# Softmax attention and linear attention on one core: another mark for the zero matmuls, the last normalisation ahead of the leftover steps, and VectorE's blocks at other places

## The chip, the core and the metric

One core of a Trainium2 chip runs the whole program: TensorE (PE in the profile) multiplies matrices, ScalarE (ACT) takes exponentials, VectorE (DVE) and GpSimd (POOL) do elementwise work, SyncE (SP) issues most of the transfers. The metric is the device time of one execution in microseconds (us). The kernel before takes 875.0 us, the median of 3 runs from 873.52 to 875.77.

## The reference

Two independent blocks with the same shapes, 2048 rows of 640 features, 32 heads of 20:

```python
qkv = (x @ wqkv)  ->  q, k, v per head
# A: softmax attention
p = softmax(q k^T * 20 ** -0.5);  o = p v;  a = o @ wo
# B: linear attention
phi(t) = where(t > 0, t + 1, exp(t)) + 1e-6
kv = phi(k)^T v;  z = sum(phi(k));  o = phi(q) kv / (phi(q) z + 1e-6);  b = o @ wo
out = concatenate([a, b], axis=-1)
```

All inputs and the output are bf16.

## The kernel before

**The units of A.** Block A is cut into 32 pieces n: 8 groups g of four heads, times 4 chunks of 512 queries (n = 4 g + chunk). Each n has 16 key tiles kt of 128 keys, and each tile four heads i, so that a unit (n, kt, i) is one score matmul (line 1193): 20 features by 128 keys by 512 queries, in one quarter of TensorE's rows, into one of the eight banks of TensorE's result memory (`ps`, 512 columns each). Its exponential is taken in one of two ways.

- On ScalarE: `emit_exp` (line 1250, the instruction is line 1259) takes three units at once from banks 0 to 2, then two from banks 3 and 4, in turn, and writes them to `f_PT`. There are 730 such groups; group j is the counter of the whole program.
- On VectorE: `ND[n]` says how many of the 16 key tiles of n go there, 56 in all. `d_score` (line 1281) evicts a score from bank 6 or 7 with a scale and an offset (line 1294); three polynomial passes over two units (lines 1305, 1309, 1313) give the exponential in `f_PD`. One key tile, a block, is four evictions and six passes.

**The output of A.** `pv_quad` (line 1344) multiplies the four exponentials of a key tile with `f_V` into bank 5 (`PVB`), four matmuls side by side, each in a quarter of the columns; 16 of them add up there for one n. A column of ones in `f_V` gives the sums. `norm` (line 1403) then transposes the bank on VectorE (line 1407), takes reciprocals (1414), multiplies on GpSimd (1417; for the last n on VectorE, 1420) and transposes back into `f_OTp` (1424); transfers (line 1436) lay it into `f_OTd`, from which `step_out` multiplies with `wo`. For the last n, `norm` keeps reciprocal, product and transposition in `self.norm_last`.

**The background.** Everything else is a list of steps: projections of A (`step_qk`, `step_v`), the whole of B (`b_steps`), and the output of A (`step_out`). A step takes bank 6 or 7, issues its matmuls piece by piece, and ends with an eviction. `bg` (line 985) issues pieces for as long as the planned end of TensorE's work lies ahead of `limit`, the planned end of the exponential of group j plus 0.12 us. Without credit it goes on only where `recent`, the planner's TensorE work in the last 3.41 us (a quarter of the array counts a quarter), is not above `FLOOR`.

**The planner.** All instructions are put in order while the program is built. `_Clock` (line 728) is a clock kept by hand with fixed costs; `run` (line 1832) goes through the 730 groups: scores of group j+1, a score for VectorE, exponential j, `emit_pv`, `bg`, `fill`, then whatever VectorE has left.

**The zero matmuls.** `zeros` (line 1197) puts a matmul with zero weights (`f_z`) beside the scores, in a quarter of the rows. `fill` (line 1216) puts sets of four, each in a quarter of the columns, up to 512 wide, into bank 5, where zeros add nothing. It stops when the room up to `limit` is used, or when `recent` is above `FLOOR`, and it does nothing where no product of the present n stands in bank 5 yet or where the bank isn't free. It runs for 2 < j < 725.

**The end.** `tail` (line 1942) issues the last products, then all steps that are left over; `finish_out` (line 1493) then issues products of `f_OTd` and `wo` (`part1`), calls `norm_last`, multiplies the last `f_OTp` with the last rows of `wo` (`part2`), adds on VectorE (line 1540) or copies on ScalarE (line 1536), and stores.

Of the kernel before, what the change touches and what calls it, by code (L numbers as in the profile page):

```python
# [5 lines left out]
F32 = mybir.dt.float32  # L6
# [793 lines left out]
class _Fast:  # L800
# [3 lines left out]
    AUX = (6, 7)  # L804
    NPT = 20
    NPD = 8
    FLOOR = 1.45
    GAP = 0.2
    BURST = True
    LEAD = 0.6  # L810
    LATE = ((3, 1), (3, 0), (2, 1))
    ND = (1, 2, 1, 1, 2, 2, 2, 2, 2, 2, 2, 2, 2, 2, 1, 2, 2, 2, 2, 2, 2, 1, 2, 1, 2, 2, 2, 2, 2, 1, 1, 2)
    OCT = 42
    EXP_A = -65536.0
    EXP_B = 3.8973859448844363 * 65536.0
# [4 lines left out]
    def __init__(self, nc, sch, es, ps, A_x, A_wqkv, A_wo, B_x, B_wqkv, B_wo, out):  # L820
        self.nc = nc
        self.sch = sch
        self.es = es
        self.ps = ps
        self.Ax, self.Aw, self.Awo = A_x, A_wqkv, A_wo
        self.Bx, self.Bw, self.Bwo = B_x, B_wqkv, B_wo
        self.out = out[0]
        self.S = A_x.shape[1]
        self.NQC = self.S // 512
        self.NT = self.S // 128  # L830
        self.prio = []
        self.qa = []
        self.qb = []
        self.qv = []
        self.done = {}
        self.cur = None
        self.open = set()
        self.ck = sch.clock = _Clock()
        self.acts = []
        self.dq = []  # L840
        self.last_chain, self.last_n = None, -1
        self.nq = []
        self.credit = 0
        self.j = -1
        self.brr = 0
        self.zj = {}
        self.aslot = self.bslot = 0
        self.hlo = []
        for c in range(N_DC):
            h0 = (128 * c) // D_HEAD  # L850
            h1 = min(N_HEADS - 1, (128 * c + 127) // D_HEAD)
            self.hlo.append((h0, h1 - h0 + 1))
# [4 lines left out]
    def alloc(self):  # L857
        S, NT = self.S, self.NT
        self.KT = self.sb("f_KT", [128, 2, S], BF16)
        self.Qr = self.sb("f_Qr", [128, 4, 512], BF16)  # L860
        self.V = self.sb("f_V", [128, NT, N_HEADS, 21], BF16)
        self.xT = self.sb("f_xT", [128, N_DC, S], BF16)
        self.wA = self.sb("f_wA", [128, N_DC, 3 * D_MODEL], BF16)
        self.wo = self.wA[:, :, 2 * D_MODEL:3 * D_MODEL]
        self.wo7 = self.sb("f_wo7", [128, D_MODEL], BF16)
        self.PT = self.sb("f_PT", [128, self.NPT, 512], BF16)
        self.PD = self.sb("f_PD", [128, self.NPD, 512], BF16)
        self.W = self.sb("f_W", [128, 2, 1024], F32)
        self.PL = self.sb("f_PL", [128, 2, 1024], F32)
        self.T1 = self.sb("f_T1", [128, 512], F32)  # L870
        self.Tn = self.sb("f_Tn", [128, 512], BF16)
        self.OTp = self.sb("f_OTp", [128, 512], BF16)
        self.R = self.sb("f_R", [128, 32], F32)
        self.OTd = self.sb("f_OTd", [128, N_DC, S], BF16)
        self.stage = self.sb("f_st", [128, 4, D_MODEL], BF16)
        self.wBq = self.sb("f_wBq", [128, N_DC, D_MODEL], BF16)
        self.wBkv = self.sb("f_wBkv", [128, N_DC, 2 * D_MODEL], BF16)
        self.woB = self.wBkv[:, :, 0:D_MODEL]
        self.pqT = self.wBkv[:, :, D_MODEL:D_MODEL + 512]
        self.xBt = self.sb("f_xB", [128, 2, N_DC, 512], BF16)  # L880
        self.xB = [self.xBt[:, k] for k in range(2)]
# [12 lines left out]
        self.Cs = self.sb("f_cs", [128, 2, 128], BF16)  # L894
        self.De = self.sb("f_de", [128, 16, 21], BF16)
        self.rd = self.sb("f_rd", [128, 2, 16], F32)
        self.Z = self.sb("f_z", [128, 128], BF16)
        self.G = self.sb("f_g", [128, 128], BF16)
        self.gmx = self.sb("f_gmx", [128, 8], F32)
        self.ident = self.sb("f_id", [128, 128], BF16)  # L900
        self.flag = self.sb("f_flag", [128, 1], I32)
        self.bmx = self.sb("f_bmx", [128, 1], F32)
        self.warm = self.sb("f_warm", [128, 1], F32)
        self.ones = self.sb("f_ones", [128, 1], F32)
# [309 lines left out]
                        self.G[32 * i:32 * (i + 1), :].unsqueeze(1).broadcast_to([32, 4, 128]), start=False, stop=False, reads=("Z", "G"), writes=(("ps", b),), tp=(32 * i, 0), inc=False, sgc=True)  # L1214

    def fill(self, limit):
        while self.pvcnt[min(self.pvn, self.NN - 1)] > 0:
            t = self.ck.pe_end()
            w = int(2400 * (limit - t - 0.1)) // 128 * 128
            if w <= 0 or self.ck.recent(limit) > self.FLOOR:  # L1220
                return
            if self.sch.when((), (("ps", self.PVB),), skip="pe") > t:
                return
            w = min(w, 512)
            for i in range(4):
                self.sch.mm(self.ps[32 * i:32 * (i + 1), self.PVB, 0:w], self.Z[:, 32 * i:32 * (i + 1)],
                            self.G[:].unsqueeze(1).broadcast_to([128, w // 128, 128]), start=False, stop=False, reads=("Z", "G"),
                            writes=(("ps", self.PVB),), tp=(0, 32 * i), inc=False, sgc=True)

    def force_qk(self, n, kt):  # L1230
        g, qc = divmod(n, self.NQC)
# [32 lines left out]
    def d_ready(self, slack):  # L1264
        k = self.dk
        if k >= len(self.dun):
            return None
        p = k // 2
        if p >= 2 and self.dC.get(p - 2) is None:
            return None  # L1270
        return self.bank(slack)

# [8 lines left out]
    def d_score(self, b):  # L1281
        sch, ps = self.sch, self.ps
        k = self.dk
        i = self.d_head()
        self.dk += 1
        n, kt, _ = self.dun[k]
        self.dhead.setdefault(k // 4, []).append(i)
        p, h = divmod(k, 2)
        x = p % 2
        self.score(b, n, kt, i, True)  # L1290
        cs = 128.0 / (LN2 * float(D_HEAD) ** 0.5)
        cb = 128.0 * (127 + self.OCT)
        dst = self.W[:, x, 512 * h:512 * (h + 1)]
        self.dve(0.69, lambda e: e.tensor_scalar(dst, ps[:, b, :], cs, cb, op0=ALU.mult, op1=ALU.add),  # L1294
                 reads=(("ps", b),), writes=(("W", x, h),))
        if h == 0:
            return
        w, pl = self.W[:, x, :], self.PL[:, x, :]
# [77 lines left out]
    def emit_pv(self, most, limit, last=False):  # L1376
        c = 0
        while c < most and self.pvn < self.NN:
# [8 lines left out]
            if left_d and self.pvcnt[n] > 0:  # L1387
                cj = self.dC.get(2 * self.pdnext + 1)
                if cj is not None and cj <= t:
                    self.pv_d()  # L1390
                    c += 1
                    continue
            if left_d and self.pvcnt[n] >= self.NT - 2 and (ok_a or not left_a):
                self.d_force(self.pdnext)
                self.pv_d()
                c += 1
                continue
# [5 lines left out]
    def norm(self, n):  # L1403
# [46 lines left out]
        if n == self.NN - 4:  # L1450
            for t in range(4 * (self.NQC - 1), 4 * self.NQC):
                for h in range(2):
                    if (t % 4, h) not in self.LATE:
                        self.prio.append(self.step_out(t, h, 1, (("OT", n), ("bkv", self.NQC - 1, 3))))

    def step_out(self, t, h, part, needs):
        sch, ps = self.sch, self.ps
        tl = t % 4
# [8 lines left out]
        def post(b):  # L1467
# [8 lines left out]
            if h == 0:  # L1476
                self.aslot ^= 1
            s = self.aslot
            dst = self.stage[:, s, cs]
            self.dve(0.49, lambda e: e.tensor_copy(dst, ps[:, b, 0:320]), reads=(("ps", b),),  # L1480
                     writes=(("stage", s, h),))
            if h == 1:
                sch.dma("sp", lambda e: e.dma_start(self.out[128 * t:128 * (t + 1), 0:D_MODEL],
                                                    self.stage[:, s, :]),
# [8 lines left out]
    def finish_out(self):  # L1493
# [15 lines left out]
                     self.wo7[:, 320 * h:320 * (h + 1)], x not in late, True, w7, banks[x], True)  # L1509
        for x in late[:2]:  # L1510
            part1(x)
        n = self.NN - 1
        self.norm_last(n)
        for x in tiles[:len(tiles) - len(late)]:
            part2(x)
        for x in late[:2]:
# [58 lines left out]
    def b_steps(self):  # L1575
# [162 lines left out]
        def ostep(t, h):  # L1738
# [8 lines left out]
            def post(b):  # L1747
                if h == 0:
                    self.bslot ^= 1
                s = 2 + self.bslot  # L1750
                dst = self.stage[:, s, 320 * h:320 * (h + 1)]
                self.dve(0.49, lambda e: e.tensor_copy(dst, ps[:, b, 0:320]), reads=(("ps", b),),  # L1752
                         writes=(("stage", s, h),))
                if h == 1:
                    sch.dma("sp", lambda e: e.dma_start(
                        self.out[128 * t:128 * (t + 1), D_MODEL:2 * D_MODEL], self.stage[:, s, :]),
                        reads=(("stage", s, 0), ("stage", s, 1)), writes=(("bout", t),))
# [184 lines left out]
    def tail(self, NG):  # L1942
        nq = len(self.quads)
        self.udone = 4 * nq
        while self.pvn < self.NN:
            self.j += 1
            self.run_acts(1e9)
            if self.pvn == self.NN - 1 and self.pvcnt[self.pvn] == self.NT - 1:
                while self.nq or self.dq:
                    if self.nq:  # L1950
                        self.nq.pop(0)[1]()
                    else:
                        self.d_pass()
            self.emit_pv(1, 1e9, True)
        while self.cur is not None or self.prio or self.qa or self.qv or self.qb or self.nq:
            self.j += 1
            self.run_acts(1e9)
# [91 lines left out]
```

## Time and profile before

| | |
|---|---|
| timed runs | 875.0 us (873.52 to 875.77) |
| the profiled execution | 870.45 us, its span 868.6 us |
| ScalarE busy | 850.2 us, 790 instructions |
| TensorE busy | 757.8 us, 11260 matmuls |
| VectorE busy | 751.2 us, 1036 instructions |
| mean granted TensorE clock | 0.996 |
| first exponential begins, last ends | 10.7 and 858.2 us |

The span runs from the first to the last instruction of one execution. A row of a group reads: line, engine, operation, written tile <- read tiles, shapes, count, then busy time in us and mean ns of one, then idle time of the engine just before these instructions and what ended it. A row of a stretch reads: from:to, its length, then the busy time of PE, PEld (weight load), DVE, ACT and POOL with counts, the granted clock, the share of the transfer engines and GB/s. A row of the chain reads start, length, engine, tile, line; one of the timeline start, length, engine, line, operation.

### The profile page before, as it was taken

How to read it: one execution, taken by the hardware profiler on the slowest of the kernel's cores; microseconds unless marked ns; L12 is line 12 of the kernel's file. 1: busy time of each engine (PE TensorE's matmuls, PEld its weight loads, DVE VectorE, ACT ScalarE, POOL GpSimd, SP SyncE). 2: the span in 40 equal slices, each digit the busy share in tenths (PEclk: the TensorE clock that was granted, in tenths of full speed). 3: DMA queues.
4: the chain of work that ended last, by engine and by line, in shares of the span. 5: the costliest groups of instructions: out<-in, count | busy, mean ns of one | idle time of the engine just before them, and what ended most of it. 6: DMA issues, size and time to landing. Idle time of an engine off the chain costs nothing.

```text
span 868.6 us, 24858 instructions
## 1 busy us (share of the span) xinstructions
PE 757.8 (87%) x11260; PEld 274.7 (32%) x11260; DVE 751.2 (86%) x1036; ACT 850.2 (98%) x790; POOL 48.5 (6%) x54
## 2 busy tenths in 40 slices
PE   8988888888888888888888988888988898899987
PEld 3333323222233233333332333233322332233333
DVE  6897689999998999988989999979879989898785
ACT  6999999999999999999999999999999999999995
POOL 4000000000000000000000000000000000000000
PEclk9999999999999999999999999999999999999999
DMA  7920100000110001000020000200010000001002
GB/s 129 239 55 5 35 3 4 5 6 5 36 43 2 5 6 36 5 2 5 6 72 6 5 11 19 43 5 14 28 32 5 5 22 21 2 5 44 21 31 79
DMA packets 45745, 23.98 MB, mean 28 GB/s; under 512 B 33984, under 2 KB 44992, under 8 KB 45632
## 3 DMA queue, kind: packets, MB, share of 16 engines
q1 hardware_dynamic: 44176, 21.92, 10.3%
q8 instruction: 90, 1.47, 0.7%
q10 hardware_dynamic: 1456, 0.40, 0.2%
q14 instruction: 23, 0.19, 0.1%
HBM read 7.31 MB, written 5.24 MB: 14 GB/s over the span
## 4 chain that ended last, share of the span: by engine, by line
ACT 95%; PE 3%; DVE 0%; DMA 0%; SPq 0%; issue 0%; ACTq 0%
ACT f_PT L1259 93%; PE ps L179 3%; ACT f_ex L1560 2%; DMA f_OTd<-f_OTp 0%; SPq L1436 0%; ACT f_st L1536 0%; PE ps L1067 0%; DVE f_OTp L1424 0%; DVE f_KT L1161 0%; PE ps L1724 0%; DVE f_Tn L1420 0%; DVE f_pk L1734 0%; DVE f_OTp L1038 0%; DVE f_st L1752 0%; ACTq L1527 0%
## 5 line engine op out<-in xcount | busy, mean ns | idle before, releaser
L1259 ACT ACTIVATE f_PT<-ps 128x1536 bf16<-128x1536 f32 x730 | 841.7, 1428 | 3.4 <-PE ps L179 3.3
L179 PE MATMUL ps<-f_Qr,f_KT 20*128 20x512 bf16 x2048 | 303.0, 385 | 103.0 <-ACT f_PT L1259 93.8
L1294 DVE TENSOR_SCALAR f_W<-ps 128x512 f32<-128x512 f32 x224 | 153.9, 687 | 52.5 <-PE ps L179 49.8
L179 PE MATMUL ps<-f_g,f_z 32*128 32x512 bf16 (+2 forms) x744 | 187.1, 384 | 0.0
L179 PEld LDWEIGHTS ps<-f_Qr,f_KT 20*128 20x128 bf16 x2048 | 75.0, 91 | 342.4 <-ACT f_PT L1259 325.8
L179 PE MATMUL ps<-f_PT,f_V 128*21 128x512 bf16 x1824 | 180.3, 387 | 0.6 <-issue 0.3
L1309 DVE SCALAR_TENSOR_TENSOR f_PL<-f_W,f_PL 128x1024 f32<-128x1024 uint16 x112 | 135.6, 1212 | 1.1
L1305 DVE SCALAR_TENSOR_TENSOR f_PL<-f_W 128x1024 f32<-128x1024 uint16 x112 | 135.6, 1213 | 0.9
L1313 DVE SCALAR_TENSOR_TENSOR f_PD<-f_PL,f_W 128x1024 uint16<-128x1024 f32 x112 | 135.6, 1211 | 0.4
L179 PE MATMUL ps<-f_xT,f_wA 128*32 128x512 bf16 x1280 | 88.4, 380 | 0.0
L1417 POOL TENSOR_TENSOR f_Tn<-f_T,f_R 128x320 bf16<-128x320 f32 x31 | 38.8, 1251 | 787.0 <-DVE f_R L1414 787.0
L179 PEld LDWEIGHTS ps<-f_PT,f_V 128*21 128x21 bf16 x1824 | 44.5, 89 | 102.1 <-issue 100.4
L179 PE MATMUL ps<-f_wBkv,f_xB 128*32 128x320 bf16 x1280 | 61.0, 307 | 0.0
L179 PEld LDWEIGHTS ps<-f_g,f_z 32*128 32x128 bf16 (+1 forms) x744 | 45.1, 92 | 8.2 <-issue 6.3
L179 PEld LDWEIGHTS ps<-f_xT,f_wA 128*32 128x32 bf16 x1280 | 30.3, 96 | 30.1 <-issue 9.0
L1560 ACT ACTIVATE f_ex<-ps 128x320 f32<-128x320 f32 (+1 forms) x52 | 36.9, 709 | 0.0
L179 PEld LDWEIGHTS ps<-f_wBkv,f_xB 128*32 128x32 bf16 x1280 | 30.5, 97 | 19.4 <-issue 7.4
L179 PE MATMUL ps<-f_wA,f_OTd 128*32 128x320 bf16 (+1 forms) x640 | 30.9, 301 | 0.4 <-DMA f_OTd<-f_OTp 0.4
L179 PE MATMUL ps<-f_wA,f_xT 128*32 128x160 bf16 (+1 forms) x640 | 30.2, 301 | 0.5 <-DVE f_Qr L1165 0.3
L179 PE MATMUL ps<-f_wBkv,f_pk 128*32 128x320 bf16 x640 | 30.6, 300 | 0.0
L179 PE MATMUL ps<-f_kvm,f_cs 128*32 128x336 bf16 x384 | 29.2, 306 | 0.0
L179 PE MATMUL ps<-f_kvm,f_wBkv 128*32 128x336 bf16 x384 | 29.1, 308 | 0.0
(89 smaller groups left out, 507.3 us busy)
## 6 DMA issues: line engine op xcount, KB each, us to landing
out_dram<-f_st SPq DMA_DIRECT2D x31, 160.0 KB
f_OTd<-f_OTp SPq DMA_DIRECT2D x108, 20.0 KB
f_wBkv<-in_B_wqkv_dram SPq DMA_DIRECT2D x1, 1600.0 KB
f_wA<-in_A_wqkv_dram SPq DMA_DIRECT2D x2, 685.0 KB
f_wBq<-in_B_wqkv_dram SPq DMA_DIRECT2D x1, 800.0 KB
f_wA<-in_A_wo_dram SPq DMA_DIRECT2D x1, 800.0 KB
f_wBkv<-in_B_wo_dram SPq DMA_DIRECT2D x1, 800.0 KB
f_st<-in_A_x_dram SPq DMA_DIRECT2D x2, 320.0 KB
```

What stands on the lines that cost most here:

```text
L179: lambda e: e.matmul(out, lhsT, rhs, start=start, stop=stop, tile_position=tp, skip_group_check=sgc),
L1259: sch.op("act", lambda e: e.activation(self.PT[:, s0:s0 + n, :], ps[:, b0:b0 + n, :], AF.Exp, bias=(self.OCT + self.EXP_S) * LN2, scale=sc ...
L1294: self.dve(0.69, lambda e: e.tensor_scalar(dst, ps[:, b, :], cs, cb, op0=ALU.mult, op1=ALU.add), reads=(("ps", b),), writes=(("W", x, h),))
L1305: self.dve(1.24, lambda e: e.scalar_tensor_tensor(pl, lo, self.EXP_A, lo, op0=ALU.add, op1=ALU.mult), reads=rw, writes=(("PL", x),), fill= ...
L1309: self.dve(1.24, lambda e: e.scalar_tensor_tensor(pl, lo, self.EXP_B, pl, op0=ALU.add, op1=ALU.mult), reads=rw, writes=(("PL", x),), fill= ...
L1313: self.dve(1.24, lambda e: e.scalar_tensor_tensor(pd, pl, self.EXP_K, w, op0=ALU.mult, op1=ALU.add), reads=rw + (("PL", x),), writes=(("PD ...
L1417: sch.op("pool", lambda e: e.tensor_tensor(n3[:, :, 0:D_HEAD], t3[:, :, 0:D_HEAD], rb, op=ALU.mult), reads=("T1", ("R", n % 2)), writes=(" ...
L1560: sch.op("act", lambda e: e.activation(ex, src, AF.Exp, bias=-1.0), reads=(("ps", b),), writes=(("ex", k),), cost=0.05 + 0.00084 * n)
```

## The change

The mark goes from 1.45 to 1.7 us. `fill` no longer stops where bank 5 holds no product of the present n: it takes bank 5 where it may, else the bank of the step that is being issued, once its first piece is in. `norm_last` is called in `tail`, ahead of the leftover steps, and no longer in `finish_out`. From then on output copies go to ScalarE, by the new helper `evac`. `ND` moves three blocks: from n=6 to n=2, from 22 to 21, from 31 to 30. `NX` and `HOLD` are names for what was fixed before (two buffers; no holding back).

```diff
-    FLOOR = 1.45
+    NX = 2
+    FLOOR = 1.7
     GAP = 0.2
+    HOLD = False
...
-    ND = (1, 2, 1, 1, 2, 2, 2, 2, 2, 2, 2, 2, 2, 2, 1, 2, 2, 2, 2, 2, 2, 1, 2, 1, 2, 2, 2, 2, 2, 1, 1, 2)
+    ND = (1, 2, 2, 1, 2, 2, 1, 2, 2, 2, 2, 2, 2, 2, 1, 2, 2, 2, 2, 2, 2, 2, 1, 1, 2, 2, 2, 2, 2, 1, 2, 1)
...
     def fill(self, limit):
-        while self.pvcnt[min(self.pvn, self.NN - 1)] > 0:
+        while True:
             t = self.ck.pe_end()
             w = int(2400 * (limit - t - 0.1)) // 128 * 128
             if w <= 0 or self.ck.recent(limit) > self.FLOOR:
                 return
-            if self.sch.when((), (("ps", self.PVB),), skip="pe") > t:
+            banks = [self.PVB] if self.pvcnt[min(self.pvn, self.NN - 1)] > 0 else []
+            if self.cur is not None and self.cur[3] > 0 and self.cur[0].key[0] not in ("tr", "bkv", "gram", "flag"):
+                banks.append(self.cur[1])
+            banks = [b for b in banks if self.sch.when((), (("ps", b),), skip="pe") <= t]
+            if not banks:
                 return
-            w = min(w, 512)
+            b, w = banks[0], min(w, 512)
...
+    def evac(self, dst, src, reads, writes):
+        if self.ending:
+            self.sch.op("act", lambda e: e.copy(dst, src), reads=reads, writes=writes, cost=0.32)
+        else:
+            self.dve(0.49, lambda e: e.tensor_copy(dst, src), reads=reads, writes=writes)
...
-        n = self.NN - 1
-        self.norm_last(n)
         for x in tiles[:len(tiles) - len(late)]:
             part2(x)
...
             self.emit_pv(1, 1e9, True)
+        self.ending = True
+        self.norm_last(self.NN - 1)
         while self.cur is not None or self.prio or self.qa or self.qv or self.qb or self.nq:
```

The output copies of `step_out` (line 1480) and of B's output step (line 1752) call `evac` in place of `self.dve`.

More of the change, by code (lines that the diff above doesn't have):

```diff
@@ L840, in __init__ @@
         self.dq = []
+        self.ending = False
         self.last_chain, self.last_n = None, -1
@@ L867, in alloc @@
         self.PD = self.sb("f_PD", [128, self.NPD, 512], BF16)
-        self.W = self.sb("f_W", [128, 2, 1024], F32)
-        self.PL = self.sb("f_PL", [128, 2, 1024], F32)
+        self.W = self.sb("f_W", [128, self.NX, 1024], F32)
+        self.PL = self.sb("f_PL", [128, self.NX, 1024], F32)
         self.T1 = self.sb("f_T1", [128, 512], F32)
@@ L1221, in fill @@
                 return
-            if self.sch.when((), (("ps", self.PVB),), skip="pe") > t:
+            banks = [self.PVB] if self.pvcnt[min(self.pvn, self.NN - 1)] > 0 else []
[3 more added lines that the diff above has]
+            if not banks:
                 return
-            w = min(w, 512)
+            b, w = banks[0], min(w, 512)
             for i in range(4):
-                self.sch.mm(self.ps[32 * i:32 * (i + 1), self.PVB, 0:w], self.Z[:, 32 * i:32 * (i + 1)],
+                self.sch.mm(self.ps[32 * i:32 * (i + 1), b, 0:w], self.Z[:, 32 * i:32 * (i + 1)],
                             self.G[:].unsqueeze(1).broadcast_to([128, w // 128, 128]), start=False, stop=False, reads=("Z", "G"),
-                            writes=(("ps", self.PVB),), tp=(0, 32 * i), inc=False, sgc=True)
+                            writes=(("ps", b),), tp=(0, 32 * i), inc=False, sgc=True)
     def force_qk(self, n, kt):
@@ L1268, in d_ready @@
         p = k // 2
-        if p >= 2 and self.dC.get(p - 2) is None:
+        if p >= self.NX and self.dC.get(p - self.NX) is None:
             return None
@@ L1288, in d_score @@
         p, h = divmod(k, 2)
-        x = p % 2
+        x = p % self.NX
         self.score(b, n, kt, i, True)
@@ L1392, in emit_pv @@
                     continue
-            if left_d and self.pvcnt[n] >= self.NT - 2 and (ok_a or not left_a):
+            if left_d and self.pvcnt[n] >= self.NT - 2 and (ok_a or not left_a) and (last or not self.HOLD):
                 self.d_force(self.pdnext)
@@ L1479, in post @@
             dst = self.stage[:, s, cs]
-            self.dve(0.49, lambda e: e.tensor_copy(dst, ps[:, b, 0:320]), reads=(("ps", b),),
-                     writes=(("stage", s, h),))
+            self.evac(dst, ps[:, b, 0:320], (("ps", b),), (("stage", s, h),))
             if h == 1:
@@ L1751, in post @@
                 dst = self.stage[:, s, 320 * h:320 * (h + 1)]
-                self.dve(0.49, lambda e: e.tensor_copy(dst, ps[:, b, 0:320]), reads=(("ps", b),),
-                         writes=(("stage", s, h),))
+                self.evac(dst, ps[:, b, 0:320], (("ps", b),), (("stage", s, h),))
                 if h == 1:
```

## The prediction

> **What bounds the kernel now.** I read the page first (busy times, the chain that ended last), then ScalarE's own waits, then the busy time in 40 equal stretches and in single clock windows, and last the timeline of the final 14 us.
>
> ```profile
> span 868.6 us, 24858 instructions
> PE 757.8 (87%) x11260; PEld 274.7 (32%) x11260; DVE 751.2 (86%) x1036; ACT 850.2 (98%) x790; POOL 48.5 (6%) x54
> ...
> ACT 95%; PE 3%; DVE 0%; DMA 0%; SPq 0%; issue 0%; ACTq 0%
> ...
> L1259 ACT ACTIVATE f_PT<-ps 128x1536 bf16<-128x1536 f32 x730 | 841.7, 1428 | 3.4 <-PE ps L179 3.3
> L179 PE MATMUL ps<-f_Qr,f_KT 20*128 20x512 bf16 x2048 | 303.0, 385 | 103.0 <-ACT f_PT L1259 93.8
> L1294 DVE TENSOR_SCALAR f_W<-ps 128x512 f32<-128x512 f32 x224 | 153.9, 687 | 52.5 <-PE ps L179 49.8
> ...
> L1305 DVE SCALAR_TENSOR_TENSOR f_PL<-f_W 128x1024 f32<-128x1024 uint16 x112 | 135.6, 1213 | 0.9
> ```
>
> ```profile
> ACT f_PT L1259 <- PE ps L179: 3.3, 6, 1.9
> ```
>
> ScalarE is busy for 98% of the span and makes 95% of the last chain, nearly all of it the 730 exponentials of line 1259. Their idle time is 3.4 us in total; the wait row (total, times, longest) has 1.9 us of it in one piece, ahead of the first exponential. TensorE's score matmuls (f_Qr,f_KT) waited 103.0 us, 93.8 of them for ScalarE: TensorE runs ahead and is held back. So there is time to win in three places only: the start, the few gaps between exponentials, and what follows the last one. The chain in order of time gives the pace of the exponentials and the end:
>
> ```profile
> 389.57 61.13 ACT f_PT L1259 x54
> ...
> 849.59 8.62 ACT f_PT L1259 x8
> ...
> 858.25 1.76 PE ps L179 x43
> ...
> 860.04 0.49 DVE f_st L1752
> 860.53 0.17 DVE f_R L1414
> ...
> 861.25 0.72 DVE f_OTp L1424
> 861.97 0.04 issue
> 862.01 1.03 PE ps L179 x24
> ```
>
> An unbroken run takes 61.13 / 54 = 1.132 us for an exponential of 2.5 score blocks on average. The diff leaves the sum of VectorE's blocks at 56 and the order of the exponentials has 730 in both programs, so this floor, 730 x 1.132 = 826 us and those of problem B beside them, stays.
>
> **The gaps, and the higher mark.** Stretches of the clock's own length around two drops:
>
> ```profile
> 274.56:277.97 3.41, 2.38 (x27) 0.63 (x27) 3.38 (x5) 3.41 (x6) 0.00 (x0) 1.00 0.00 0
> 277.97:281.38 3.41, 3.41 (x42) 1.08 (x38) 2.59 (x6) 2.93 (x4) 0.32 (x1) 0.50 0.00 0
> ...
> 380.37:383.78 3.41, 2.40 (x35) 0.65 (x27) 2.53 (x5) 3.41 (x5) 0.00 (x0) 1.00 0.00 0
> 383.78:387.20 3.42, 3.42 (x38) 0.91 (x35) 2.03 (x5) 3.12 (x4) 0.00 (x0) 0.50 0.02 5
> 387.20:390.61 3.41, 3.41 (x41) 1.76 (x38) 3.41 (x5) 3.23 (x3) 1.58 (x1) 1.00 0.00 0
> ```
>
> The columns are PE, PEld, DVE, ACT and POOL busy, then the granted clock. In two stretches of 3.41 us the clock is 0.50, and there alone in mid-kernel does ScalarE lose time: 3.41 - 2.93 = 0.48 us in the first, and (3.42 - 3.12) + (3.41 - 3.23) = 0.48 us around the second. One drop costs 0.48 us; both, 0.96. What came ahead is not an idle TensorE (2.38 and 2.40 of 3.41 us busy), but a thin one. The groups of matmuls in the stretch ahead of the first drop (274.56 to 277.97) and then those in a thin stretch of the same grid that no drop followed (527.14 to 530.55):
>
> ```profile
> L179 PE MATMUL ps<-f_Qr,f_KT 20*128 20x512 bf16 x10 | 1.6, 382 | 1.0 <-ACT f_PT L1259 1.0
> L179 PE MATMUL ps<-f_PT,f_V 128*21 128x512 bf16 x8 | 0.9, 428 | 0.0
> L179 PE MATMUL ps<-f_g,f_z 128*32 128x512 bf16 x4 | 0.4, 390 | 0.0
> L179 PE MATMUL ps<-f_g,f_z 32*128 32x512 bf16 x1 | 0.4, 385 | 0.0
> L179 PE MATMUL ps<-f_c,f_cs 128*32 128x320 bf16 x4 | 0.3, 299 | 0.0
> ...
> L179 PE MATMUL ps<-f_Qr,f_KT 20*128 20x512 bf16 x12 | 1.8, 384 | 0.9 <-ACT f_PT L1259 0.9
> L179 PE MATMUL ps<-f_g,f_z 32*128 32x512 bf16 x3 | 1.2, 385 | 0.0
> L179 PE MATMUL ps<-f_xT,f_wA 128*32 128x512 bf16 x12 | 1.0, 382 | 0.0
> L179 PE MATMUL ps<-f_PT,f_V 128*21 128x512 bf16 x8 | 0.8, 386 | 0.0
> ```
>
> All of these use a quarter of the array (20 or 32 rows, or 21 or 32 columns), so I count quarter-matmuls of 512 columns: 10 + 8 + 4 + 1 + 4 x 320/512 = 25.5 ahead of the drop, and 12 + 3 + 12 + 8 = 35 in the stretch that had none. The limit lies somewhere between. What one costs:
>
> ```profile
> 835.17 0.40 PE L179 MATMUL ps<-f_PT,f_V 128*21 128x512 bf16 x4
> ...
> 835.39 0.39 PE L179 MATMUL ps<-f_PD,f_V 128*21 128x512 bf16 x4
> ```
>
> Four of them side by side start 835.39 - 835.17 = 0.22 us after the four before, so one counts 0.055 us. The planner's mark of 1.45 us is 26 of them in its window of 3.41 us, about where the clock fell; 1.7 us is 31, inside the gap between the two.
>
> The Trainium skill (TensorE: Matmul & The Clock Gate, Part 1) has the window too, 3413 ns and free-running, with half the clock as the only lower state. The two stretches of 3.41 us at 0.50 agree. But it lets the clock fall after an idle window, and by that rule nothing would be gained here by zeros; the trace speaks against it, since both windows ahead were 70% busy.
>
> How much of it goes? In the program's order the diff adds 252 zero matmuls of the four-column kind (244 before, 496 after: 63 sets more). I laid the array work that stands between successive exponentials in each order along the exponentials' measured pace and slid a window of 3.41 us over it. Under 1.40 us lie 1.1% of the window positions before and 0.7% after: of some 250 windows, 2.7 and 1.8 (the profiled run had 2). So the thin places get fewer but do not go: in the rest neither the output bank nor a step's bank is free to write to, or the work is thin because a score waits. Value taken: 0.9 drops x 0.48 = **0.4 us**; bounds 0 (each drop comes back elsewhere) and 0.96 (both go, none comes).
>
> **What the zeros cost.** 63 x 0.22 = 13.9 us of TensorE. It is put where TensorE waits for ScalarE (the 93.8 us above) and ends by the plan 0.1 us ahead of the limit. A set that overruns has this cover:
>
> ```profile
> 841.58 0.39 PE L179 MATMUL ps<-f_Qr,f_KT 20*128 20x512 bf16 x3 [0.21 <-ACT f_PT L1259]
> ```
>
> These scores begin about 0.2 us after an exponential has freed their banks and take 0.39: they are there 0.6 us after it ended, and are needed one exponential later, 0.9 (two blocks) to 1.35 us (three). 0.3 to 0.75 us are spare, more than one set of zeros. I take 0. Bounds: 0, and 13.9 us if every set pushes its exponential in full.
>
> **The end.** In the chain above VectorE first copies two output halves of problem B (line 1752; the second runs 860.04 to 860.53) and then begins line 1414, the reciprocal of the last head group. The eviction it needs was done earlier:
>
> ```profile
> 858.68 0.72 DVE L1407 STREAM_TRANSPOSE f_T<-ps 128x512 f32<-128x512 f32 x1 [0.63 <-PE ps L179]
> 859.42 1.10 DVE L1752 CAST f_st<-ps 128x320 bf16<-128x320 f32 x2
> ...
> 863.15 0.75 ACT L1536 CAST f_st<-ps 128x320 bf16<-128x320 f32 x2 [4.95 <-PE ps L179]
> ```
>
> After the change the reciprocal stands right behind the transposition on VectorE, at 859.42: 860.53 - 859.42 = **1.1 us** earlier, and the product, the second transposition and the last matmuls follow at their old distances. Is something else late then? On TensorE the 40 matmuls of wA,f_OTd stood behind 40 of problem B's output; in the new order those 40 come before the last scores, so the 40 of f_OTd can start about 858.5, and with 10 sets of 0.14 to 0.16 us (43 matmuls in 1.76 us) are through by 860.2. The new OTp is there at 861.97 - 1.1 = 860.87. TensorE is ready, 1.1 us stands. Bounds 0.4 (TensorE becomes late) and 1.1.
>
> The copies on ScalarE, which the new helper would make after the last exponential, are in neither program: ScalarE's order has the same instructions in both, because in the new order no step of problem B is left over. That edit is worth 0. (The three copies of line 1536 show ScalarE's price, 0.4 us.) The new NX and HOLD have the values that make them idle.
>
> **The 56 blocks.** Three move: from n=6 to 2, 22 to 21, 31 to 30. A block is 4 evictions and 6 polynomial passes, 4 x 0.687 + 6 x 1.21 = 10.0 us of VectorE, and spares ScalarE four score blocks, 4 x 1.132 / 2.5 = 1.8 us, in its own n and gives them back in the other. No sum changes. At some 26 us for one n, n=2 lies at 63 to 90 us, 6 at 168 to 194, 21 and 22 at 566 to 617, 30 and 31 from 805:
>
> ```profile
> 65.10:86.80 21.70, 18.49 (x283) 6.67 (x275) 16.85 (x24) 21.70 (x22) 0.73 (x1) 1.00 0.02 5
> 86.80:108.50 21.70, 18.37 (x260) 7.84 (x261) 13.14 (x20) 21.70 (x22) 0.73 (x1) 1.00 0.18 36
> ...
> 564.20:585.90 21.70, 18.80 (x292) 6.58 (x289) 16.16 (x25) 21.70 (x22) 0.73 (x1) 1.00 0.02 5
> ...
> 802.90:824.60 21.70, 21.39 (x373) 8.51 (x373) 15.22 (x25) 21.70 (x21) 0.73 (x1) 1.00 0.07 23
> ```
>
> VectorE is idle for 4.9 + 8.6 us around n=2, 5.5 at n=21 and 6.5 at n=30, so the blocks go to where it has room. I take 0; bounds: 0.5 us gained (what is left of the 3.4 us of idle time, without the 1.9 at the start and the 0.96, goes), 3.6 lost (one pass of 1.2 us late at each of three places).
>
> **The sum.** The profiled execution took 870.45 us, 1.8 more than its span of 868.6. Minus 1.1 and 0.4 gives 868.95. The median of the timed runs is 875.0 (873.52 to 875.77), 4.55 above the profiled one; I cannot place that difference, and take the gain over: 875.0 - 1.5 = **873.5**. A difference under 0.3%, 2.6 us, is about what a measurement of this kernel cannot tell from no change.
>
> **Rivals.** (1) *The timed runs drop more often.* The windows of the clock stand anywhere against the program, and by my sliding count a run may meet one to eight thin ones. If the 4.55 us are drops at 0.48 (up to nine) and the mark removes two thirds, the gain is 1.1 + 3.0 = 4.1 us: about 871. For it: the spread of the timed runs, 2.25 us. Against: half of my thin places stay. (2) *The zeros get in the way.* Where the plan's clock is late against ScalarE's by more than the 0.3 us spare behind a two-block exponential, every added set there delays the exponential by up to 0.22 us; if this holds for half of the 63, 6.9 us are lost and 1.5 won: about 880. Against: with 61 sets in the program already, the exponentials idle for only 0.5 us outside the start and the drops. (3) *Given back.* A block of VectorE comes late at its new place (1.2 us), or the thinner end (no zeros in the last five groups, 40 matmuls fewer behind them) gets a drop that slows the last matmuls: 1.03 us becomes 2.06. Either takes the 1.1 us: about 875.
>
> **Chances.** My forecast 0.52 (its own range 872 to 875), rival 1 0.25, rival 2 0.08, rival 3 0.15. The range that leaves out some 2 in 10 goes from 870.3 (most of rival 1) to 876.2 (most of rival 3, hardly any of rival 2). Faster by over 0.3%, under 872.4: 0.23 of rival 1 and 0.09 of mine, 0.32. Slower by over 0.3%, over 877.6: rival 2 and 0.02 of rival 3, 0.10. Within: 0.58.
>
> **What will show it.** The last chain after the last exponential: reciprocal right behind the transposition, no copy between, and 9.3 us from the last exponential to the end of the span instead of 868.6 - 858.2 = 10.4. Stretches at clock 0.50: none or one. Idle time ahead of line 1259's exponentials: 0.4 us less. Wrong would be gaps at clock 1.00 (rival 2, with TensorE's zeros as the last thing ahead of the scores; rival 3, with VectorE or a late f_PD ahead), or as many drops as before.

## The result: 872.4 us, and the profile after

The changed kernel takes 872.38 us (median of 22 runs, 870.01 to 874.58), the kernel before 875.55 us in the same runs. The ratio is 0.9959, with a 95% interval from 0.9942 to 0.9976: 0.4% faster, 3.2 us by the medians. One of the 22 runs of the kernel before took 1087.56 us, and the ratio leaves it out. The result is inside the stated range and more than the likeliest case of 1.5 us. The profiled execution took 870.36 us, only 0.1 less than that of before.

The page of the changed kernel, its busy times, its chain and three groups:

```profile
span 868.5 us, 25388 instructions
PE 767.9 (88%) x11524; PEld 278.2 (32%) x11524; DVE 751.0 (86%) x1036; ACT 850.1 (98%) x790; POOL 50.9 (6%) x54
...
ACT 95%; PE 4%; DVE 0%; issue 0%; ACTq 0%
...
L1266 ACT ACTIVATE f_PT<-ps 128x1536 bf16<-128x1536 f32 x730 | 841.4, 1423 | 3.6 <-PE ps L179 3.6
L179 PE MATMUL ps<-f_Qr,f_KT 20*128 20x512 bf16 x2048 | 302.6, 385 | 91.6 <-ACT f_PT L1266 82.3
L179 PE MATMUL ps<-f_g,f_z 32*128 32x512 bf16 (+3 forms) x1008 | 208.5, 378 | 0.0
```

1008 matmuls of zeros in place of 744, and TensorE's wait for ScalarE is 11.5 us shorter (82.3 against 93.8): the zeros went where TensorE waited. ScalarE has as much to do as before, and its exponentials idle no less (3.6 us, 3.4 before). So this pair of profiles does not show the gain. What it does show is one stretch at half clock (three stretches of the clock's length; the columns are PE, PEld, DVE, ACT, POOL, then the clock):

```profile
66.01:69.42 3.41, 2.78 (x38) 0.82 (x30) 3.20 (x5) 3.41 (x5) 0.00 (x0) 1.00 0.00 0
69.42:72.83 3.41, 3.41 (x38) 1.12 (x35) 2.70 (x6) 2.65 (x4) 1.58 (x1) 0.50 0.00 0
72.83:76.24 3.41, 2.99 (x51) 1.10 (x47) 3.02 (x6) 3.41 (x4) 0.00 (x0) 1.00 0.09 23
```

Here it cost ScalarE 3.41 - 2.65 = 0.76 us. The chain's end, from the last exponential on:

```profile
858.16 0.40 PE ps L179
858.56 0.02 issue
858.59 0.73 DVE f_T L1414
859.31 0.02 issue
859.34 0.27 DVE f_R L1421
859.60 0.02 issue
859.63 0.50 DVE f_Tn L1427
860.13 0.02 issue
860.15 0.72 DVE f_OTp L1431
860.87 0.04 issue
860.92 1.03 PE ps L179 x24
```

The reciprocal follows the transposition, and the last matmuls begin at 860.92, where 860.9 was predicted.

**The timed runs.** Every timed run comes with its span and mean granted clock, and from these follows how many stretches it spent at half clock: (1 - clock) x span / 1.707 us, since a stretch of 3.413 us at 0.50 lacks half of itself. Beside the first four experiments, 25 runs of the kernel before have 2.0 to 10.8 such stretches, 7.2 in the median, and their times follow: 868.3 us + 1.23 us for each, with a correlation of 0.97. The 22 runs of the changed kernel have 0.5 to 5.1, 2.0 in the median: 870.0 us + 0.94 us for each. The profiled execution of before was one with two. The count also takes in a drop behind the last copy: in the profile of the zeros' mark 2.0 below, whose clock is 0.998, the last 3.7 us alone are at half clock.

### The profile page after: what moved, and what is told of

The parts are those of the page before. It is cut to its first block, busy times and chain, and to the rows that moved or that the text cites. A ratio compares the mean times of both kernels' runs of the same rounds, so it can differ in the third digit from the quotient of the medians.

```text
span 868.5 us, 25388 instructions
## 1 busy us (share of the span) xinstructions
PE 767.9 (88%) x11524; PEld 278.2 (32%) x11524; DVE 751.0 (86%) x1036; ACT 850.1 (98%) x790; POOL 50.9 (6%) x54
## 4 chain that ended last, share of the span: by engine, by line
ACT 95%; PE 4%; DVE 0%; issue 0%; ACTq 0%
ACT f_PT L1266 93%; PE ps L179 4%; ACT f_ex L1570 2%; ACT f_st L1546 0%; PE ps L1070 0%; DVE f_T L1414 0%; DVE f_OTp L1431 0%; DVE f_KT L1164 0%; DVE f_Tn L1427 0%; DVE f_OTp L1041 0%; ACTq L1537 0%; DVE f_KT L1162 0%; DVE f_R L1421 0%; DVE f_warm L1040 0%; ACTq L104 0%
## 5 line engine op out<-in xcount | busy, mean ns | idle before, releaser
L179 PE MATMUL ps<-f_Qr,f_KT 20*128 20x512 bf16 x2048 | 302.6, 385 | 91.6 <-ACT f_PT L1266 82.3
L179 PE MATMUL ps<-f_g,f_z 32*128 32x512 bf16 (+3 forms) x1008 | 208.5, 378 | 0.0
L1424 POOL TENSOR_TENSOR f_Tn<-f_T,f_R 128x320 bf16<-128x320 f32 x31 | 41.3, 1331 | 782.8 <-DVE f_R L1421 782.8
L179 PEld LDWEIGHTS ps<-f_g,f_z 128*32 128x32 bf16 (+1 forms) x1008 | 51.4, 93 | 12.5 <-issue 8.8
L1467 DVE CAST f_st<-ps 128x320 bf16<-128x320 f32 x56 | 27.2, 487 | 13.9 <-PE ps L179 12.7
L179 PE MATMUL ps<-f_wA,f_xT 128*32 128x160 bf16 (+1 forms) x640 | 29.6, 301 | 0.4
```

The source lines that it names most:

```text
L179: lambda e: e.matmul(out, lhsT, rhs, start=start, stop=stop, tile_position=tp, skip_group_check=sgc),
L1424: sch.op("pool", lambda e: e.tensor_tensor(n3[:, :, 0:D_HEAD], t3[:, :, 0:D_HEAD], rb, op=ALU.mult), reads=("T1", ("R", n % 2)), writes=(" ...
L1467: self.dve(0.49, lambda e: e.tensor_copy(dst, src), reads=reads, writes=writes)
```

## The experiments

Each ran beside the kernel before, five rounds. "Stretches" is the median over its timed runs. The base is the difference from before at the same number of stretches, from one slope fitted to both, with its 95% interval.

| kernel | us | ratio to before | stretches (before) | base, us |
|---|---|---|---|---|
| the mark alone | 871.08 | 0.9931 [0.9903, 0.9958] | 1.3 (7.2) | +1.1 +- 1.0 |
| the end alone | 875.79 | 0.9986 [0.9952, 1.002] | 6.7 (7.2) | -0.2 +- 0.7 |
| the blocks alone | 892.83 | 1.0172 [1.0127, 1.0217] | 20.4 (7.2) | +0.4 +- 1.7 |
| the change, mark 2.0 | 880.89 | 1.0039 [1.0014, 1.0063] | 4.6 (7.2) | +6.4 +- 0.6 |
| the mark, one zero matmul of four | 871.69 | 0.9941 [0.9912, 0.997] | 2.0 (7.7) | -0.1 +- 0.9 |
| the mark and the end | 870.88 | 0.9927 [0.9899, 0.9956] | 1.3 (7.7) | -0.3 +- 0.9 |
| the change again | 871.33 | 0.9937 [0.9911, 0.9962] | 2.0 (7.7) | -0.6 +- 0.9 |
| the mark 1.85 and the end | 881.51 | 1.0062 [1.0035, 1.0088] | 6.2 (7.7) | +5.6 +- 0.6 |
| the mark, no zeros issued | 899.82 | 1.0247 [1.0197, 1.0297] | 25.5 (7.7) | +1.1 +- 2.8 |
| zeros' mark 1.7, steps' mark 1.45 | 872.30 | 0.9937 [0.9915, 0.996] | 2.0 (7.7) | +1.4 +- 1.3 |
| zeros' mark 2.0, steps' mark 1.45 | 870.16 | 0.9915 [0.9883, 0.9946] | 0.5 (7.7) | +1.2 +- 1.6 |
| zeros' mark 1.45, steps' mark 1.7 | 887.13 | 1.0113 [1.0074, 1.0151] | 11.2 (7.7) | +5.4 +- 1.2 |

The base of the change again leaves out one of its nine runs: it took 874.1 us at a mean clock of 0.942, which would be 29.6 stretches, far off the line. Why is open.

**The three parts, one at a time.** The mark alone is the changed `fill` in the kernel before:

```diff
-    FLOOR = 1.45
+    FLOOR = 1.7
```

> The kernel before with the higher mark (1.7) and zeros into a step's open bank alone: 123 sets of zeros instead of 61, the old blocks, the old end. If the gain of the change lies in fewer stretches at half clock (A), this kernel gains 2 to 4 us over the kernel before, its timed runs show a mean clock about 0.005 to 0.008 higher than before's, and the time over all runs rises by about 0.9 us for each stretch of 3.41 us at 0.50. If the end carries the gain (B), it gains at most 1 us. If the blocks' new places carry it (C), it gains nothing.

It won 0.69%, with 1.3 stretches. The new `fill` may also write to a step's bank, but it never does: without the new bank, the mark alone and the changed kernel each have the same instructions in the same order, and the new `fill` at the old mark of 1.45 gives the instructions of the kernel before. All zeros of `fill` in the changed kernel go into bank 5.

The end alone:

```diff
+        self.ending = True
+        self.norm_last(self.NN - 1)
         while self.cur is not None or self.prio or self.qa or self.qv or self.qb or self.nq:
...
-        n = self.NN - 1
-        self.norm_last(n)
```

> The kernel before with the early normalisation and the ScalarE copies alone; 40 matmuls and two copies of problem B are left over behind the last product, as before, and the copies go to ScalarE. Under A and C it stays within 1 us of before: the last matmuls begin 1.1 us earlier, but most of that is lost again while the last stores land (after's last copy ended 1.1 us earlier and its span only 0.1). Under B it is 1.1 us or more faster, and the span behind the last exponential falls from 10.4 to 9.3 us.

In the timed runs this is nothing that can be told from 0. The chain of its profile says why so little could come:

```profile
859.72 4.39 PE ps L179 x104
864.12 0.02 issue
864.14 0.02 ACTq L104
864.16 0.04 issue
864.20 0.76 ACT f_st L1542 x2
```

With the 40 leftover matmuls in place, TensorE itself makes the end: 40 + 40 + 24 matmuls in one piece. Its last exponential ended at 859.68, so the ScalarE copies begin 4.5 us behind it, against 863.15 - 858.21 = 4.9 in the kernel before and 862.03 - 858.12 = 3.9 in the changed one, where no step is left over. From the last exponential to the last copy it is 6.6 us in six of the seven profiles with the old blocks and the old end (6.9 in the one with lone zeros), 6.2 in all three with the old blocks and the early normalisation, 5.9 with the blocks alone, and 5.6 in the changed kernel. So the early normalisation gives 0.4 us here, and the full step needs the blocks' move too.

The blocks alone:

```diff
-    ND = (1, 2, 1, 1, 2, 2, 2, 2, 2, 2, 2, 2, 2, 2, 1, 2, 2, 2, 2, 2, 2, 1, 2, 1, 2, 2, 2, 2, 2, 1, 1, 2)
+    ND = (1, 2, 2, 1, 2, 2, 1, 2, 2, 2, 2, 2, 2, 2, 1, 2, 2, 2, 2, 2, 2, 2, 1, 1, 2, 2, 2, 2, 2, 1, 2, 1)
```

> The kernel before with the three blocks at their new places alone: the planner then places 42 sets of zeros (61 before), and 28 leftover matmuls come late instead of 40. Under A the time follows the number of stretches at half clock, so within 1.5 us of before in either direction, more likely above it. Under C it is 2 us or more faster.

None of the three theories has the size: 15.5 us slower by the medians, with 20 stretches at half clock. They come in strings, here one of eight (the second line is the whole string):

```profile
382.57:385.98 3.41, 2.25 (x34) 0.59 (x22) 2.33 (x5) 3.41 (x6) 0.00 (x0) 1.00 0.00 0
385.98:413.29 27.31, 27.31 (x201) 11.32 (x197) 17.65 (x28) 19.71 (x18) 0.73 (x1) 0.50 0.02 4
413.29:416.70 3.41, 3.41 (x48) 1.32 (x45) 2.51 (x5) 3.41 (x3) 0.00 (x0) 1.00 0.00 0
```

TensorE is busy for the whole 27.31 us, at half clock, and ScalarE for 19.71 of them: 7.6 us lost, 0.95 for each stretch. A stretch in this string costs more than the single 0.48 us of the profile before. Why this plan is so much thinner stays open; it has 42 sets of zeros, before has 61. Blocks of VectorE also come late in it, as the third rival of the prediction feared: TensorE's products wait for them three times, at 612, 775 and 801 us, 3.8 us in all. In the profiles of before and of the changed kernel they never do.

**More zeros in the changed plan.**

```diff
-    FLOOR = 1.7
+    FLOOR = 2.0
```

> The changed kernel with the mark at 2.0: 245 sets of zeros (124 in the changed kernel). Under A a further 1 to 2 us are won and the mean clock in the timed runs rises above 0.998. If zeros cost TensorE's time ahead of the scores (the rival of the prediction), it is slower than the changed kernel, by up to 0.22 us for each set that pushes an exponential, with gaps between exponentials at clock 1.00.

It is slower than the kernel before, by 0.39%, and by its base of +6.4 us, not by its clock. Its profile shows two places for that. TensorE's products wait twice for a late block of VectorE, 3.0 us in all, and more work is left over for the end, as two pieces of its last chain show:

```profile
860.96 2.75 PE ps L179 x52
...
866.84 4.19 PE ps L179 x104
```

From the last exponential to the last copy it takes 9.1 us, where the changed kernel takes 5.6. The mark at 1.85 on the plan with the old blocks loses as much:

```diff
-    FLOOR = 1.7
+    FLOOR = 1.85
...
-    ND = (1, 2, 2, 1, 2, 2, 1, 2, 2, 2, 2, 2, 2, 2, 1, 2, 2, 2, 2, 2, 2, 2, 1, 1, 2, 2, 2, 2, 2, 1, 2, 1)
+    ND = (1, 2, 1, 1, 2, 2, 2, 2, 2, 2, 2, 2, 2, 2, 1, 2, 2, 2, 2, 2, 2, 1, 2, 1, 2, 2, 2, 2, 2, 1, 1, 2)
```

> The kernel with the mark and the early normalisation, the blocks at their old places, with the mark at 1.85: 173 sets of zeros against 123. At 2.0 the changed kernel lost, with VectorE's blocks late in the profile and a base of 876 us. If more zeros still remove stretches at half clock without such waits, 870 us or less; if the loss at 2.0 comes on gradually, 872 to 876 us with fewer than 2 stretches at half clock.

The loss came at once and not gradually. Here the end is not longer (6.2 us), but TensorE's products wait three times for a late block, 7.8 us in all. The longest, in four lines of the timeline around 547 us:

```profile
544.58 0.39 PE L179 MATMUL ps<-f_PD,f_V 128*21 128x512 bf16 x2
...
547.05 1.22 DVE L1320 SCALAR_TENSOR_TENSOR f_PD<-f_PL,f_W 128x1024 uint16<-128x1024 f32 x1
...
548.32 0.60 PE L179 MATMUL ps<-f_PD,f_V 128*21 128x512 bf16 x2 [3.34 <-DVE f_PD L1320]
548.85 0.60 PE L179 MATMUL ps<-f_Qr,f_KT 20*128 20x512 bf16 x1
```

The product of a VectorE block stands in TensorE's order before the block is done. Two of its four matmuls run, the other two wait 3.34 us for the last pass, and the scores behind them wait too; ScalarE then idles 3.2 us. TensorE, busy for 1.07 of the 3.42 us from 543.90 on, drops its clock on top.

**What the clock counts.** The same plan as the mark alone, with one matmul of each set issued, and then with none:

```diff
+            t = self.sch.when(("Z", "G"), (("ps", b),), skip="pe")
             for i in range(4):
+                if i > 0:
+                    self.ck.step("pe", t, ("c", 32 * i, w))
+                    continue
                 self.sch.mm(self.ps[32 * i:32 * (i + 1), b, 0:w], self.Z[:, 32 * i:32 * (i + 1)],
```

> The kernel with the higher mark alone (871.1 us, about 1.3 stretches at half clock in a timed run), but of each set of four zero matmuls only the first is issued, at the same place in the same order; the planner still counts four. TensorE is busy for nearly as long, but the sets fill a quarter of the array's columns in place of all. If the clock follows the share of the array at work (my count in quarter-matmuls), the thin places are thinner than in the kernel before: more than 7 stretches at half clock in a timed run, and 878 to 890 us. If it follows TensorE's busy time, the result is that of the four: 1 to 2 stretches, 871 us.

```diff
+            t = self.sch.when(("Z", "G"), (("ps", b),), skip="pe")
             for i in range(4):
-                self.sch.mm(self.ps[32 * i:32 * (i + 1), b, 0:w], self.Z[:, 32 * i:32 * (i + 1)],
...
+                self.ck.step("pe", t, ("c", 32 * i, w))
```

> The kernel with the higher mark alone, its planner counting 123 sets of zero matmuls as before, but none of them issued: all other instructions stand in the same order. If TensorE's work by the zeros keeps the clock up (A), the thin places are bare: more than 10 stretches at half clock in a timed run, 880 us or more. If the mark's other use helps, the earlier start of steps, 1 to 2 stretches remain and the time is 871 us.

With none issued there are 25.5 stretches and 899.8 us, so it is TensorE's work by the zeros that keeps the clock. With one of four there are 2.0 stretches and 871.7 us, as good as four. The count by the array's share fell here. A stretch of that profile, at the place where the kernel before had its first drop:

```profile
L179 PE MATMUL ps<-f_Qr,f_KT 20*128 20x512 bf16 x10 | 1.6, 382 | 0.6 <-ACT f_PT L1270 0.5
L179 PE MATMUL ps<-f_g,f_z 128*32 128x512 bf16 x3 | 0.8, 383 | 0.0
L179 PE MATMUL ps<-f_PT,f_V 128*21 128x512 bf16 x8 | 0.8, 383 | 0.0
L179 PE MATMUL ps<-f_g,f_z 32*128 32x512 bf16 x1 | 0.4, 385 | 0.0
L179 PE MATMUL ps<-f_wBkv,f_xB 128*32 128x320 bf16 x4 | 0.3, 299 | 0.0
L179 PE MATMUL ps<-f_c,f_cs 128*32 128x320 bf16 x4 | 0.3, 299 | 0.0
...
277.57:280.99 3.42, 3.20 (x58) 1.19 (x58) 3.42 (x6) 3.42 (x4) 0.90 (x1) 1.00 0.00 0
```

The matmuls ahead of the drop at 69.42 us in the changed kernel were these:

```profile
L179 PE MATMUL ps<-f_Qr,f_KT 20*128 20x512 bf16 x12 | 2.1, 386 | 0.6 <-ACT f_PT L1266 0.6
L179 PE MATMUL ps<-f_wBkv,f_xB 128*32 128x320 bf16 x16 | 0.9, 302 | 0.0
L179 PE MATMUL ps<-f_g,f_z 32*128 32x512 bf16 x2 | 0.8, 391 | 0.0
L179 PE MATMUL ps<-f_PT,f_V 128*21 128x512 bf16 x4 | 0.4, 386 | 0.0
L179 PE MATMUL ps<-f_c,f_cs 128*32 128x320 bf16 x4 | 0.3, 299 | 0.0
```

The first is 10 + 3 + 8 + 1 + 2.5 + 2.5 = 27 quarter-matmuls, and the next stretch stays at 1.00. The second is 12 + 10 + 2 + 4 + 2.5 = 30.5, and the clock fell. These rows count whole what only reaches into a stretch. With such matmuls shared between both stretches, and 0.053 us for a quarter-matmul of 512 columns, the order is the same: 1.16 us against 1.37. If a lone matmul of 128 rows by 32 columns counts as a whole one, the 27 become 36 and the 1.16 becomes 1.64. TensorE's busy time alone, the other branch of the expectation, does not sort the stretches either: of those at full clock with less than 2.4 us of it, over all 14 profiles, 34 were followed by a drop and 65 were not. What exactly the clock counts stays open.

**Which mark.** `FLOOR` is used twice: by the zeros and by the start of steps. The next two split it, in the kernel of the mark alone:

```diff
-            if (self.cur is None or not self.BURST) and self.credit <= 0 and self.ck.recent(self.ck.pe_end()) > self.FLOOR:
+            if (self.cur is None or not self.BURST) and self.credit <= 0 and self.ck.recent(self.ck.pe_end()) > 1.45:
...
-            if w <= 0 or self.ck.recent(limit) > self.FLOOR:
+            if w <= 0 or self.ck.recent(limit) > 1.7:
```

> The kernel before with the mark at 1.7 for the zeros and at 1.45 for the start of steps: 124 sets of zeros, and the other matmuls in nearly the order of the kernel before. Under A it has the full gain: 1 to 2 stretches at half clock and 870 to 872 us. If the gain needs the steps' mark, it stays at 875 us or above with 5 or more stretches.

```diff
+            if (self.cur is None or not self.BURST) and self.credit <= 0 and self.ck.recent(self.ck.pe_end()) > 1.7:
...
+            if w <= 0 or self.ck.recent(limit) > 1.45:
```

> The other split: steps start by the mark of 1.7, the zeros keep 1.45 (44 sets, 61 before). Under A no gain: 5 or more stretches at half clock, 875 us or above, and a higher base if blocks come late. If the steps' mark carries the gain, 871 us.

The zeros' mark alone has the whole gain; the steps' mark alone costs 1.1%, with 11 stretches and a base of +5.4 us. Its profile has late blocks too. The waits (total, times, longest) of its exponentials and of TensorE's products read:

```profile
ACT f_PT L1266 <- PE ps L179: 16.1, 18, 3.6
...
PE ps L179 <- DVE f_PD L1320: 7.2, 4, 3.9
```

The profiles of the mark alone and of the zeros' mark 1.7 have no such wait for `f_PD`. So steps that start by a higher mark can make the blocks late, with fewer zeros than before. They don't always: in the mark alone the steps have 1.7 as well, and its base is +1.1 us. `recent` counts the zeros too, so more zeros may hold the steps back there; that is not shown. Whether zeros alone make blocks late was tested with still more zeros and the steps as before, 2.0 and 1.45:

```diff
-            if (self.cur is None or not self.BURST) and self.credit <= 0 and self.ck.recent(self.ck.pe_end()) > self.FLOOR:
+            if (self.cur is None or not self.BURST) and self.credit <= 0 and self.ck.recent(self.ck.pe_end()) > 1.45:
...
-            if w <= 0 or self.ck.recent(limit) > self.FLOOR:
+            if w <= 0 or self.ck.recent(limit) > 2.0:
```

> The same with the zeros' mark at 2.0 and the steps' at 1.45: 239 sets. At 2.0 for both, with the blocks of the change, the base was 876 us, with products of VectorE's blocks waited for at full clock. If the zeros themselves cost TensorE's time ahead of the scores, 875 us or more with a base near that. If the steps' mark makes the blocks late, 869 to 871 us, with at most one stretch at half clock.

It has the lowest median of all, 870.16 us, with 239 sets, nearly as many as the 245 that lost at 2.0, though on the old blocks and with the old end. Its profile has no late block and no stretch at half clock between 5 and 865 us:

```profile
span 869.2 us, 26282 instructions
...
PE 793.8 (91%) x11972; PEld 286.9 (33%) x11972; DVE 753.7 (87%) x1036; ACT 849.9 (98%) x790; POOL 48.4 (6%) x54
...
L1266 ACT ACTIVATE f_PT<-ps 128x1536 bf16<-128x1536 f32 x730 | 841.5, 1432 | 3.1 <-PE ps L179 3.0
```

Its runs spread from 869.4 to 871.0, those of the kernel before beside it from 872.5 to 882.3. Its ratio lies below the changed kernel's (0.9959 and 0.9937), but the intervals overlap.

**The blocks within the change.** The mark and the end with the old blocks, and the changed kernel as it is:

```diff
-    ND = (1, 2, 2, 1, 2, 2, 1, 2, 2, 2, 2, 2, 2, 2, 1, 2, 2, 2, 2, 2, 2, 2, 1, 1, 2, 2, 2, 2, 2, 1, 2, 1)
+    ND = (1, 2, 1, 1, 2, 2, 2, 2, 2, 2, 2, 2, 2, 2, 1, 2, 2, 2, 2, 2, 2, 1, 2, 1, 2, 2, 2, 2, 2, 1, 1, 2)
```

> The changed kernel with the blocks at their old places: the higher mark and the early normalisation. If the gain is the mark's alone (A) and the blocks cost a little, 870 to 871.5 us, the same as the mark alone and up to 1.5 us under the changed kernel in the same session. If the end is worth its 1.1 us (B), 870 us or less. If the blocks belong to the gain (C), 1 us or more above the changed kernel.

> The changed kernel, as it is, beside the others on one chip: 872.4 us in its first session, with 2 stretches at half clock in the median timed run. The same is expected, within 1 us.

They took 870.88 and 871.33 us, no difference that could be told. Inside the changed plan the blocks' places make none that these runs show; alone they cost 15.5 us.

## Why the prediction was right, and where its sum was not

**The number.** The range and the direction held. That the sum came near is in part luck: its larger term, 1.1 us for the end, cannot be seen in the timed runs, and its smaller one, 0.4 us for the gaps, carries the gain. "Within 0.3%" was given 0.58 and "faster by over 0.3%" 0.32; the measured 0.41%, with an interval from 0.24 to 0.58, lies mostly in the second.

**The gaps.** Place and sign were right, the size was not. The term "0.9 drops x 0.48 = 0.4 us" should have been about five drops at 0.9 to 1.2 us; the medians differ by 3.2 us at first and by 5.4 where the change ran again (876.71 and 871.33). Three things were mis-sized in it.

First, the two drops of the profiled execution were taken for the usual number; the timed runs have 7.

Second, the limit was taken for 1.40 us. Over the stretches of 12 profiles (all but the one with lone zeros and the one with no drop), counted by quarters of the array with the matmuls at an edge shared, 41 of 44 below 1.40 us were followed by a drop, 12 of 37 from there to 1.49, and none of 2777 above. How an edge is shared moves this by a few: another way gives 43 of 47, 10 of 32 and none of 2780. The stretch that the prediction took for safe, with 35 quarter-matmuls, has 1.45 us when its edges are shared, so it lay on the limit too, and the one ahead of the first drop 1.18. With 1.46 us, a value inside the band, a window slid over the matmuls of the profile before finds 6.6 thin places (2 to 10, by where it begins), and after 1.8 (0 to 4), near the medians of the timed runs (7.2 and 2.0).

Third, the price was read from two single drops. Drops also come in strings, as in the second profile of the changed kernel:

```profile
247.56:250.97 3.41, 2.71 (x31) 0.81 (x28) 2.10 (x5) 3.41 (x4) 0.00 (x0) 1.00 0.00 0
250.97:254.39 3.42, 3.42 (x23) 1.55 (x20) 2.35 (x4) 2.87 (x3) 0.00 (x0) 0.50 0.00 0
254.39:257.80 3.41, 3.41 (x30) 0.96 (x28) 2.79 (x6) 2.89 (x3) 1.14 (x1) 0.50 0.00 0
257.80:261.21 3.41, 3.41 (x42) 1.10 (x39) 2.22 (x3) 2.85 (x3) 0.44 (x1) 0.50 0.03 7
261.21:264.63 3.42, 3.42 (x59) 1.25 (x56) 2.69 (x4) 3.14 (x4) 0.00 (x0) 1.00 0.09 22
```

These three cost ScalarE 0.55, 0.52 and 0.56 us, and 0.28 more in the stretch behind them. Over whole profiles without late blocks, ScalarE's idle time in and just behind such stretches is between 0.4 us for each (this profile) and 1.0 (33 stretches, no zeros issued). So strings can cost more, but no profile of the kernel before shows why its timed runs pay 1.23 us for each; that stays open.

So the old mark of 1.45 us lay on the limit and the new one above it. The rival "the timed runs drop more often" is what happened. It had a gain of 4.1 us, 1.1 of them from the end, against 3.2 measured by the medians; each drop costs about twice the 0.48 us that it took.

The 4.55 us between the profiled and the timed runs, which the prediction could not place, fit four to five more drops at about 1 us; the clock of those three runs is not on record.

The Trainium skill (TensorE: Matmul & The Clock Gate, Part 1) calls the window free-running and, at a kernel's start, the count of cold matmuls different from run to run. The runs agree, and in mid-kernel too: the kernel before has between 1.0 and 10.8 such stretches in its timed runs.

**What the zeros cost.** Taken as 0, and 178 more sets than before cost nothing that could be seen between the exponentials (3.1 us idle with 239 sets, 3.4 with 61). A base of -0.6 to 1.4 us for the kernels with the zeros' mark raised and no late blocks, seen in some pairs and not in others, stays open.

**The end.** The step itself came true: 1.1 us, down to the last copy (863.71 after, 864.82 before). The span did not follow: from the last exponential to its end it still takes 10.4 us, where 9.3 was predicted, because the piece from the last copy on went from 3.8 to 868.52 - 863.71 = 4.8 us. In the other profiles that piece lies between 3.5 us (the mark alone) and 4.8 us (the zeros' mark at 2.0 with the old end), so it differs from one execution to the next by as much as the edit could win. Over timed runs the end alone is worth 0.2 +- 0.7 us. How much of the 1.1 us reaches the end in the changed plan was not settled. The earlier call alone brings the last copy 0.4 us nearer, the lower bound of the prediction, because 40 matmuls are left over there. The 1.1 us needs the blocks' move as well, which leaves no step over; the prediction read that order rightly but put the whole step down to the normalisation.

**The blocks.** "No sum changes" held inside the change; alone the move would have been 15 us off. A thinner plan for TensorE in mid-kernel was not among the bounds.

**Reading of the diff.** The prediction left it possible that zeros go into a step's open bank; they never do.

## What to carry to other kernels

Where another engine sets the pace and TensorE waits for it, as here, TensorE's clock can hang on how much it does in each stretch of 3.4 us, and filler in its waiting time can keep the clock up; give the filler a limit of its own and leave the plan of the real work alone. One profile holds one draw of the clock's window: read the mean clock of every timed run, and fit the time against it, before a difference is put down to an edit. A mark that lies on the limit, as 1.45 us did here, leaves no room for a plan whose times are a little off; set it above.

## What the runs showed of the hardware

- The clock fell after stretches in which TensorE was far from idle (busy for 2.38 and 2.40 of 3.41 us before, 2.78 after). The limit lies between about 1.40 and 1.49 us of work in 3.41, where four quarter-matmuls side by side count once (41 of 44, 12 of 37, 0 of 2777).
- Zeros count as work (25.5 stretches at half clock without them, 1.3 with them), and a lone matmul of 128 rows by 32 columns counts for much more than a quarter, about like four side by side: 13 stretches of the kernel with lone zeros were below 1.42 us by the array's share, and none was followed by a drop.
- The clock does not always come back after one stretch. In the same 12 profiles, a stretch at half clock with less than 2.57 us of work, counted at the doubled length that a matmul has there, was always followed by another; with more than 2.86 us never; between them both occur. In matmuls that is about what the clock needs not to fall (1.29 to 1.43 us at full clock, against 1.40 to 1.49), but at half clock TensorE takes twice as long for them: in the string of eight it was busy the whole time. So a drop can hold on to itself.
